# Operands fetched from DRAM by GpSimd's own transfers, and a work planner with durations read from a trace

## The chip, the cores and the metric

One core of one Trainium2 chip runs the whole program. The metric is the device time of one execution in microseconds (us); the time of a kernel is the median of its runs.

## The reference

Inputs are q, k, v of shape (4, 8, 576, 64) and six weights. All are float64 in DRAM; the kernel reads them as pairs of 32-bit words and makes float32 of them.

```python
scores = scale * q @ k.T + bias[h] * (-|i - j|), kept where 0 <= i - j < 128
attn   = softmax(scores);  x = (attn @ v), heads side by side: (4, 576, 512)
xn     = (x - mean(x)) / sqrt(var(x) + 1e-6) * g_ln
x      = x + relu(xn @ w_ch1) @ w_ch2            # 512 -> 2048 -> 512
h      = relu(x @ w_in)                          # 512 -> 1024
c      = conv over the sequence, 3 taps, one weight per channel, zero padded
out    = (h * sigmoid(c)) @ w_out                # 1024 -> 512
```

## The kernel before, in words

Attention runs first, in code written in its own order; neither it nor its order is touched. Everything behind it is put into a list of operations (`Plan.add`: engine, an assumed duration in ns, what is read and written). `Plan.issue` then simulates the list with those durations several times (`Plan.schedule`) and emits the best order it met. TensorE's operations stay in the order in which the program added them; the orders on VectorE (DVE), ScalarE (ACT), GpSimd (POOL) and the transfer queue of SyncE (SP) are the planner's. On the chip each engine goes through its own list strictly in order, so a waiting instruction holds up all behind it.

A float32 product is made of three fp32r products of a high and a low part (`PASSES`), so each operand exists as two parts: ACT writes the high part, DVE or POOL the rest. The tokens are in six groups of 384 columns. The stages after attention, by the time in the profile:

- **First layer, groups 0 and 1, about 148 to 289 us.** For each hidden block f of 128 (16 of them) TensorE makes 12 matmuls of the hidden layer (`plain_hidden`) and 12 of the projection of the block before (`project`). Meanwhile the last 20 of the 32 weight tiles are turned from float64 words into parts (`convert`, `convert_next`: one ACT and three DVE operations, ACT for the high and POOL for the low part) from a ring of three raw buffers. Between the blocks stand the statistics of later groups: `norm_turn` (four transposes of TensorE, two DVE operations) three times, then `norm_gather`: a small root on POOL (six instructions), a transpose of its result on TensorE, and a store to DRAM, from where `norm_spread` broadcasts it.
- **Groups 2 and 3 (s=1), then 4 and 5 (s=2).** Two groups and two hidden blocks make a superquad (`superquad`, eight for each s): a 2 by 2 product in seven products instead of eight ("P2" to "P7" in `QUAD`), each of six matmuls, with four places "F" at which waiting work (`fill`, mostly projections, six matmuls each) is put between them. The combined weights were stored in DRAM and stream back through nine slots of `r1` (`stream_record`). Behind each s, `second_half` makes the odd group's hidden blocks and projections. s=1 runs from about 289, s=2 from about 418 us.
- **Second layer, from about 513 us.** The same product in seven for w_in (`quad2`, 288 columns), gates on DVE and ACT, and the output products (`store_chunks`) as filling.

An operand comes back from DRAM by `fetch` (line 1251): SP transfers 256 KB into a staging buffer of `fa` (or of `h`), and ACT copies it to its place with type fp32r (line 1258). There are 96 fetches for the stream (`w1d`), 28 for w_in (`wind`) and 16 for w_out (`woutd`), 140 in all.

```python
plan.add("SP", 70, lambda: nc.sync.dma_start(stage(), src), [src], [key], nbytes=262144)
if eng == "S":
    plan.add("S", 590, lambda: S.activation(dst, stage(), AF.Copy), [key], [dst])
```

Lines named below: 989 a product of the plan, 952 and 959/967 a helper's ACT and DVE operations, 343/348/353 the three DVE steps of a conversion, 1031 and 1062 the transposes of `norm_turn` and `norm_gather`, 1052 to 1057 the root on POOL, 1157 the low part on POOL, 1258 the copy of `fetch`.

## Time and profile before

| | us |
|---|---|
| median of 3 runs | 745.91 (743.84 to 746.87) |
| the profiled execution | 745.31 |
| its span in the profile | 743.6 |
| TensorE (PE) busy in it | 716.6 |
| DVE / ACT / POOL busy | 536.8 / 476.1 / 145.8 |

Of the span and the execution's own time 1.7 us lie outside the span. PE's busy time is what its matmuls cover; the rest of the span is time in which PE waits. A view by engine says which instruction PE waited for; the time-ordered view of PE shows where.

### The profile page before, as it was taken

The page shows a single profiled execution, that of the slowest core. Times are in us where ns is not written, and L with a number is a line of the kernel's source. Part 1 is how long each engine was busy: PE and PEld are TensorE (multiplying, and loading weights), DVE is VectorE, ACT ScalarE, POOL GpSimd, SP SyncE. Part 2 cuts the span into 40 slices and gives each one's busy share as a digit, 9 for nine tenths or more (in the row PEclk, how much of TensorE's full clock was granted, in tenths as well). Part 3 has the DMA queues.
Part 4 walks back from the last instruction along what each step waited for, and adds up shares of the span by engine and source line. Part 5 has one row for each costly group of instructions (what it writes and reads, how often), then busy time and mean ns, then how long its engine had stood idle before and what let it go on. Part 6 is the DMA issues. An engine that isn't in the chain of part 4 may idle for free.

```text
span 743.6 us, 13429 instructions
## 1 busy us (share of the span) xinstructions
PE 716.6 (96%) x4704; PEld 667.4 (90%) x4704; DVE 536.8 (72%) x1073; ACT 476.1 (64%) x1190; POOL 145.8 (20%) x248
## 2 busy tenths in 40 slices
PE   8999998899899999999999999999999999999998
PEld 7777876799899999999999899999999898998887
DVE  5799999569999836555678665558468999687631
ACT  4888877545534435664556466677779977777742
POOL 1678789634631110000000000000000000000000
PEclk9999999999999999999999999999999999999999
DMA  6877765137759733877761388886704200000011
GB/s 152 183 169 172 198 157 150 42 91 220 235 186 319 226 119 100 284 263 257 227 222 40 117 275 292 290 258 206 227 15 143 86 15 29 30 29 15 29 43 57
DMA packets 122303, 114.63 MB, mean 154 GB/s; under 512 B 63552, under 2 KB 87292, under 8 KB 122236
## 3 DMA queue, kind: packets, MB, share of 16 engines
q1 hardware_dynamic: 121180, 113.52, 50.3%
q8 instruction: 37, 0.61, 0.3%
q10 hardware_dynamic: 1056, 0.26, 0.2%
q14 instruction: 30, 0.25, 0.1%
HBM read 80.70 MB, written 33.05 MB: 153 GB/s over the span
## 4 chain that ended last, share of the span: by engine, by line
PE 63%; DVE 3%; DMA 2%; ACT 2%; POOL 1%; issue 1%; SPq 0%; ACTq 0%; POOLq 0%; DVEq 0%
PE bank L989 63%; DVE fa L959 1%; DMA w1d<-r 1%; ACT fa L952 1%; DMA fa<-in_moe_w_out 1%; ACT r L1258 0%; PE bank L1031 0%; DMA h<-woutd 0%; DVE small L1039 0%; POOL small L1053 0%; DVE hhr L967 0%; DVE x L959 0%; DVE xn L967 0%; DVE xn L959 0%; DVE fa L353 0%
## 5 line engine op out<-in xcount | busy, mean ns | idle before, releaser
L989 PE MATMUL bank<-hhr,r 128*128 128x384 f32 x1152 | 214.5, 338 | 1.1 <-DVE fa L959 1.0
L989 PE MATMUL bank<-r,r 128*128 128x288 f32 (+1 forms) x1248 | 204.7, 315 | 5.2 <-ACT fa L952 4.3
L989 PEld LDWEIGHTS bank<-r,r 128*128 128x128 f32 x1248 | 193.8, 188 | 9.4 <-ACT fa L952 6.1
L989 PEld LDWEIGHTS bank<-hhr,r 128*128 128x128 f32 x1152 | 199.3, 188 | 2.3 <-DVE fa L959 1.7
L1258 ACT ACTIVATE r<-fa 128x512 fp32r<-128x512 f32 x115 | 70.6, 626 | 23.2 <-DMA fa<-w1d 9.7
L989 PE MATMUL bank<-r 128*128 128x512 f32 (+2 forms) x360 | 81.2, 370 | 0.3 <-ACT r L1258 0.3
L952 ACT ACTIVATE fa<-bank 128x288 f32<-128x288 f32 (+1 forms) x112 | 49.5, 442 | 38.1 <-PE bank L989 36.2
L989 PEld LDWEIGHTS bank<-r 128*128 128x128 f32 x360 | 64.0, 188 | 10.0 <-ACT r L1258 0.7
L989 PE MATMUL bank<-xn,r 128*128 128x384 f32 x360 | 68.5, 339 | 0.1
L989 PEld LDWEIGHTS bank<-xn,r 128*128 128x128 f32 x360 | 63.8, 191 | 0.4 <-POOL r L1157 0.4
L959 DVE TENSOR_TENSOR fa<-bank,fa 128x288 f32<-128x288 f32 (+1 forms) x88 | 43.6, 500 | 28.2 <-ACT fa L952 17.6
L732 ACT ACTIVATE pp<-ps,mn 128x128 f32<-128x128 f32 x144 | 51.2, 378 | 13.6 <-DVE mn L722 11.7
L952 ACT ACTIVATE hhr<-bank 128x384 fp32r<-128x384 f32 x46 | 22.5, 490 | 56.4 <-PE bank L989 56.0
L952 ACT ACTIVATE r<-fa 128x256 fp32r<-128x256 f32 (+2 forms) x94 | 47.6, 519 | 14.4 <-DVE fa L353 10.1
L967 DVE SCALAR_TENSOR_TENSOR fa<-fa,cw 128x576 f32<-128x576 f32 x64 | 51.1, 812 | 1.3 <-ACT fa L952 0.8
L1800 POOL MEMSET fa<- 128x1 f32 x12 | 0.8, 98 | 261.4 <-DVE fa L353 219.3
L744 POOL TENSOR_SCALAR pp<-pp,sm 128x128 f32<-128x128 f32 x72 | 42.8, 604 | 33.8 <-DVE sm L741 31.7
L766 POOL TENSOR_SCALAR_AFFINE_SELECT pt<-pc 128x512 f32<-128x512 f32 x72 | 46.9, 680 | 2.0 <-ACT pc L759 1.6
L707 PE MATMUL ps<-kt,qt 64*128 64x256 f32 x288 | 45.3, 410 | 2.0 <-ACT pp L732 1.7
L959 DVE TENSOR_TENSOR r<-fa,r 128x256 fp32r<-128x256 f32 (+1 forms) x74 | 37.7, 521 | 11.6 <-ACT r L952 9.0
L782 PE MATMUL po<-pt,rawv 128*64 128x128 f32 x544 | 37.9, 281 | 7.5 <-POOL pt L766 5.3
L989 PE MATMUL bank<-r,hhr 128*128 128x512 f32 (+1 forms) x192 | 44.5, 381 | 0.0
(135 smaller groups left out, 1086.6 us busy)
## 6 DMA issues: line engine op xcount, KB each, us to landing
fa<-w1d SPq DMA_DIRECT2D x96, 256.0 KB, 3.9
fa<-in_moe_w_ch SPq DMA_DIRECT2D x32, 512.0 KB, 4.7
w1d<-r SPq DMA_DIRECT2D x40, 256.0 KB, 3.1
wind<-r SPq DMA_DIRECT2D x28, 256.0 KB, 3.4
fa<-wind SPq DMA_DIRECT2D x19, 256.0 KB, 3.3
out<-h SPq DMA_DIRECT2D x17, 256.0 KB, 2.0
rawq<-in_q SPq DMA_DIRECT2D x32, 128.0 KB, 3.9
rawv<-in_v SPq DMA_DIRECT2D x32, 128.0 KB, 2.8
```

The source lines that it names most:

```text
L707: T.matmul(ps[:, h, u, :].rearrange("p (o j) -> p o j", o=2), lhs, rhs, start=i == 0, stop=i == 1,)
L732: S.activation(pp[:, u, h, :], sc[:, h, u], AF.Exp, bias=mn[:, h, u : u + 1], scale=-1.0, accum_out=sm[:, 0, i : i + 1],)
L744: (G if i % 2 else V).tensor_scalar(out=pp[:, i, :], in0=pp[:, i, :], scalar1=sm[:, 1, i : i + 1], scalar2=1.0, op0=ALU.mult, op1=ALU.mult,)
L766: G.affine_select(out=parts[:, i], in_=pc, compare_op=ALU.is_ge, fill=0.0, base=base, pattern=[[0, 4], [sign, P]], channel_multiplier=-sign,)
L782: T.matmul(po[h * D : (h + 1) * D, u, :], rvs[bl, pr][:, t - 1 + i, h, :], pt[:, i, 2 * u + h, :], start=i == i0, stop=i == 1,)
L952: "S", 160 + 0.84 * cols(out), lambda: S.activation(out, src, func, **kw),
L959: "V", 40 + 1.3 * cols(out), lambda: V.tensor_tensor(out=out, in0=a, in1=b, op=op),
L967: lambda: V.scalar_tensor_tensor(out=out, in0=a, scalar=sc, in1=b, op0=op0, op1=op1),
L989: T.matmul(out, lhs, rhs, start=start and n == 0, stop=stop and n == len(items) - 1, skip_group_check=True,)
L1258: plan.add("S", 590, lambda: S.activation(dst, stage(), AF.Copy), [key], [dst])
L1800: plan.add("G", 100, lambda hp=hp, c=c: G.memset(hp[:, c : c + 1], 0.0), [], [hp[:, c : c + 1]])
```

## The change

`fetch` becomes one transfer issued from GpSimd, straight from DRAM into the fp32r place. The planner gets other durations, more rounds, and due times that move an operation's needs earlier where the simulated PE stalled. The gathers stand one block later, and the turns of later groups further apart. The first eight converted tiles have a fourth raw buffer. The projection of the last blocks of group 1 and of group 3 becomes filling for the next superquad. The core of the diff:

```diff
-    def issue(self, rate=0.29, landing=1800, wait=200, rounds=6):
+    def issue(self, rate=0.29, landing=1800, wait=200, rounds=16):
...
-            at = {i: starts[i] for i in pe}
+            for i in pe:
+                push[i] *= 0.8
+            for a, b, i in stall:
+                push[i] += b - a
+            at = {i: starts[i] - push[i] for i in pe}
...
-            "V", 40 + 1.3 * cols(out), lambda: V.tensor_tensor(out=out, in0=a, in1=b, op=op),
+            "V", tt_ns(cols(out)), lambda: V.tensor_tensor(out=out, in0=a, in1=b, op=op),
...
-        plan.add("G", 1500, root, [keys], [keys])
+        plan.add("G", 2650, root, [keys], [keys])
...
-        raw = fav(n % 3 * 1024, 1024).bitcast(I32)
+        k = n % 4 if n < NRAW4 else n % 3
+        raw = fav(k * 1024 if k < 3 else 4608, 1024).bitcast(I32)
...
     def fetch(dst, src, key=None, stage=None, eng="S"):
...
-        plan.add("SP", 70, lambda: nc.sync.dma_start(stage(), src), [src], [key], nbytes=262144)
-        if eng == "S":
-            plan.add("S", 590, lambda: S.activation(dst, stage(), AF.Copy), [key], [dst])
...
+        plan.add("G", 1100, lambda: nc.gpsimd.dma_start(dst, src), [src], [dst], nbytes=262144)
...
-            for gg, f0 in ((1, 2), (2, 9)) if g == 0 else ((3, 0), (4, 5), (5, 10)):
-                if f0 <= f < f0 + GT:
-                    norm_turn(gg, f - f0, bank[7])
-                if f == f0 + GT:
+            for gg, at in ((1, (2, 3, 4, 6)), (2, (9, 11, 13, 15))) if g == 0 else (
+                (3, (0, 1, 2, 4)), (4, (5, 6, 7, 9)), (5, (10, 11, 12, 14))
+            ):
+                if f in at[:GT]:
+                    norm_turn(gg, at.index(f), bank[7])
+                if f == at[GT]:
                     norm_gather(gg, bank[7])
...
-            if last is not None:
+            if last is not None and (g, f) != (1, NF1 - 1):
...
-    for cs in ((0, 1), (2, 3)):
-        fill.append(lambda cs=cs: project(NF1 - 1, cs, False, True))
+    for f in (NF1 - 2, NF1 - 1):
+        for cs in ((0, 1), (2, 3)):
+            fill.append(lambda f=f, cs=cs: project(f, cs, False, f == NF1 - 1))
...
+            if p == 0:
+                fillers(len(fill) - 4)
...
-            for fn in second_half(3):
+            half = second_half(3)
+            for fn in half[:-4]:
                 fn()
+            fill += half[-4:]
```

**The gather of group 2 on PE.** bank_2367 to bank_2370 take the projection (hhr), bank_2371 and bank_2372 the hidden layer (xn), bank_2374 the transposes of the statistics (of x) and of the root's result (of small). Before, from the last turn on:

```order
L1031 MATMUL bank_2374<-ident,x 128x128 x4
L989 MATMUL bank_2367<-hhr,r_2363 128x384 x3
L989 MATMUL bank_2368<-hhr,r_2363 128x384 x3
L989 MATMUL bank_2369<-hhr,r_2363 128x384 x3
L989 MATMUL bank_2370<-hhr,r_2363 128x384 x3
L989 MATMUL bank_2371<-xn,r_2363 128x384 x12
L1062 MATMUL bank_2374<-ident,small 6x128
```

and now:

```order
L1055 MATMUL bank_2374<-ident,x 128x128 x4
L1008 MATMUL bank_2367<-hhr,r_2363 128x384 x3
L1008 MATMUL bank_2368<-hhr,r_2363 128x384 x3
L1008 MATMUL bank_2369<-hhr,r_2363 128x384 x3
L1008 MATMUL bank_2370<-hhr,r_2363 128x384 x3
L1008 MATMUL bank_2371<-xn,r_2363 128x384 x12
L1008 MATMUL bank_2367<-hhr,r_2363 128x384 x3
L1008 MATMUL bank_2368<-hhr,r_2363 128x384 x3
L1008 MATMUL bank_2369<-hhr,r_2363 128x384 x3
L1008 MATMUL bank_2370<-hhr,r_2363 128x384 x3
L1008 MATMUL bank_2372<-xn,r_2363 128x384 x12
L1086 MATMUL bank_2374<-ident,small 6x128
```

Between the last turn and the gather stood 24 matmuls; now 48 do. The other four gathers moved in the same way.

**The first superquad of s=2 on PE.** bank_2371, 2372 and 2373 take the seven products, the others projections. Before, the superquad had no filling:

```order
L989 MATMUL bank_2373<-r_62 128x384 x6
L989 MATMUL bank_2371<-r_2363,r_62 128x384 x12
L989 MATMUL bank_2372<-r_2363,r_62 128x384 x6
L989 MATMUL bank_2371<-r_2363,r_62 128x384 x12
L989 MATMUL bank_2372<-r_2363,r_62 128x384 x6
```

and now:

```order
L1008 MATMUL bank_2373<-r_62 128x384 x6
L1008 MATMUL bank_2371<-r_2363,r_62 128x384 x6
L1008 MATMUL bank_2367<-hhr,r_2363 128x384 x3
L1008 MATMUL bank_2368<-hhr,r_2363 128x384 x3
L1008 MATMUL bank_2369<-hhr,r_2363 128x384 x3
L1008 MATMUL bank_2370<-hhr,r_2363 128x384 x3
L1008 MATMUL bank_2371<-r_2363,r_62 128x384 x6
L1008 MATMUL bank_2372<-r_2363,r_62 128x384 x6
L1008 MATMUL bank_2371<-r_2363,r_62 128x384 x6
```

Four projections of group 3 that stood ahead of the superquad now stand in it, at its places F.

**POOL's queue at the head of the stream.** In before POOL has no transfers; small is the root of a gather, w1d a combined weight in DRAM, r_62 the tile of the slots. Now (the roots of groups 4 and 5 stand between fetches):

```order
L1279 DMA r_62<-w1d_5_2398 128x512
L1279 DMA r_62<-w1d_2_2395 128x512
L1076 TENSOR_SCALAR small<-small 128x3
L1077 TENSOR_TENSOR small<-small,mhalf 128x3
L1078 TENSOR_TENSOR small<-small 128x3
L1079 TENSOR_TENSOR small<-small 128x3
L1080 TENSOR_SCALAR small<-small 128x3
L1081 TENSOR_TENSOR small<-small 128x3
L1279 DMA r_62<-w1d_6_2399 128x512
L1279 DMA r_62<-w1d_1_2401 128x512
```

140 transfers moved from SP's queue to POOL's, and the 140 copies of line 1258 left ACT's.

## Rows read from the trace of the kernel before

**Rows 1.** The page: busy time, share of the span, instructions of each engine.

```profile
PE 716.6 (96%) x4704; PEld 667.4 (90%) x4704; DVE 536.8 (72%) x1073; ACT 476.1 (64%) x1190; POOL 145.8 (20%) x248
```

**Rows 2.** PE's waits, whole span: total us, times, longest us.

```profile
PE po L782 <- POOL pt L766: 5.3, 7, 1.3
PE bank L989 <- ACT fa L952: 4.3, 5, 1.3
PE bank L1062 <- POOL small L1057: 3.0, 3, 2.0
PE bank L989 <- DVE fa L959: 1.9, 3, 0.9
PE bank L989 <- ACT r L1258: 0.3, 1, 0.3
```

**Rows 3.** PE in order of time, first layer: start us, us, instructions [idle before].

```profile
167.35 0.27 PE L1062 MATMUL bank<-ident,small 128*6 128x128 f32 x1 [0.64 <-POOL small L1057]
...
196.12 2.24 PE L989 MATMUL bank<-xn,r 128*128 128x384 f32 x12
200.32 0.27 PE L1062 MATMUL bank<-ident,small 128*6 128x128 f32 x1 [1.96 <-POOL small L1057]
200.35 3.09 PE L989 MATMUL bank<-hhr,r 128*128 128x384 f32 x12
203.24 3.08 PE L989 MATMUL bank<-xn,r 128*128 128x384 f32 x12
206.16 2.25 PE L989 MATMUL bank<-hhr,r 128*128 128x384 f32 x12
...
255.98 0.27 PE L1062 MATMUL bank<-ident,small 128*6 128x128 f32 x1 [0.36 <-POOL small L1057]
...
297.05 2.35 PE L989 MATMUL bank<-r,r 128*128 128x384 f32 x12 [0.64 <-ACT fa L952]
```

**Rows 4.** Stretches: us, busy us of PE, PEld, DVE, ACT, POOL; granted clock, DMA share, GB/s.

```profile
180.00:200.00 20.00, 18.34 (x109) 17.66 (x107) 19.37 (x32) 10.18 (x19) 10.48 (x12) 1.00 0.73 217
...
200.00:205.00 5.00, 4.68 (x19) 4.68 (x20) 4.84 (x6) 2.53 (x5) 3.34 (x3) 0.66 0.79 245
...
460.00:480.00 20.00, 20.00 (x116) 20.00 (x116) 12.31 (x26) 14.11 (x30) 0.00 (x0) 1.00 0.88 288
...
560.00:580.00 20.00, 18.86 (x126) 18.18 (x125) 18.05 (x32) 18.44 (x38) 0.00 (x0) 1.00 0.48 141
```

**Rows 5.** DVE in order of time, start of the plan's work.

```profile
153.40 0.70 DVE L1039 BATCH_NORM_STATS2 small<-bank 128x6 f32<-128x512 f32 x1 [3.20 <-PE bank L1031]
```

**Rows 6.** PE and ACT in order of time, 420 to 588 us.

```profile
420.76 3.39 PE L989 MATMUL bank<-r,r 128*128 128x384 f32 x18 [0.58 <-ACT fa L952]
424.79 2.35 PE L989 MATMUL bank<-r,r 128*128 128x384 f32 x12 [0.64 <-ACT fa L952]
...
541.36 1.28 ACT L952 ACT_TABLE_LOAD   x1
...
543.68 1.05 PE L989 MATMUL bank<-r,r 128*128 128x288 f32 x6 [1.33 <-ACT fa L952]
...
575.25 3.49 PE L989 MATMUL bank<-r,r 128*128 128x288 f32 x24 [1.14 <-ACT fa L952]
...
583.15 1.86 PE L989 MATMUL bank<-r,r 128*128 128x288 f32 x12 [0.86 <-DVE fa L959]
...
587.64 0.98 PE L989 MATMUL bank<-r 128*128 128x512 f32 x3 [0.34 <-ACT r L1258]
```

**Rows 7.** Groups of instructions, DVE's of 300 to 600 us: busy us, mean ns, idle before.

```profile
L1258 ACT ACTIVATE r<-fa 128x512 fp32r<-128x512 f32 x115 | 70.6, 626 | 23.2 <-DMA fa<-w1d 9.7
...
L1157 POOL TENSOR_TENSOR r<-fa,r 128x512 fp32r<-128x512 f32 x20 | 27.7, 1388 | 41.8 <-ACT r L952 40.8 <-DMA fa<-in_moe_w_ch 0.9
...
L348 DVE SCALAR_TENSOR_TENSOR fa<-fa 128x512 int32<-128x512 int32 x15 | 10.3, 688 | 0.3
...
L343 DVE TENSOR_SCALAR fa<-fa 128x512 int32<-128x512 int32 x14 | 6.0, 425 | 5.0 <-ACT fa L333 5.0
```

**Rows 8.** SP's queue in order of time: one issue of a fetch (start us, us).

```profile
536.68 0.32 SPq L1256 DMA_DIRECT2D fa<-wind  x1
```

**Rows 9.** The page, DMA issues: count, KB each, median us to landing.

```profile
fa<-w1d SPq DMA_DIRECT2D x96, 256.0 KB, 3.9
```

More of the change, by code (lines that the diff above doesn't have):

```diff
@@ L77, in add, with schedule @@
         return i
-    def schedule(self, pe, at, succ, cost, rate, landing, wait):
+    def schedule(self, pe, goal, succ, cost, rate, landing, wait):
         ops = self.ops
         n = len(ops)
-        horizon = max(at.values()) + 1e5
+        horizon = max(goal.values()) + 1e5
         due = [0.0] * n
@@ L85, in schedule @@
             if ops[i]["eng"] == "T":
-                due[i] = at[i]
+                due[i] = goal[i]
             else:
@@ L118, in schedule @@
                 else:
-                    when = max(free.get(eng, 0.0), min(est[i] for i in items))
-                    soon = [i for i in items if est[i] <= when + wait]
+                    at = {i: max(est[i], dma - 3000) if ops[i]["nbytes"] else est[i] for i in items}
+                    when = max(free.get(eng, 0.0), min(at.values()))
+                    soon = [i for i in items if at[i] <= when + wait]
                     i = min(soon, key=lambda i: (due[i], i))
-                    if est[i] > when:
-                        now = [j for j in items if est[j] <= when]
+                    if at[i] > when:
+                        now = [j for j in items if at[j] <= when]
                         j = min(now, key=lambda j: (due[j], j))
-                        if when + ops[j]["ns"] <= est[i] + wait or due[i] > when + ops[j]["ns"] + 1500:
+                        if when + ops[j]["ns"] <= at[i] + wait or due[i] > when + ops[j]["ns"] + 1500:
                             i = j
-                    start = max(when, est[i])
+                    start = max(when, at[i])
                 if ops[i]["lock"]:
@@ L174, in issue @@
         best = None
+        push = {i: 0.0 for i in pe}
         for _ in range(rounds):
@@ L946, in two, with act_ns, tt_ns, stt_ns @@
         return sum(isinstance(a, list) or plan.known.get(a.tensor.name) == "sb" for a in aps) > 1
+    def act_ns(n: int, bank: bool = False):
+        return 182 + 0.79 * n if bank else 201 + 0.826 * n
+    def tt_ns(n: int):
+        return 150 + 1.045 * n
+    def stt_ns(n: int):
+        return 44 + 1.333 * n
     def act(out, src, func=AF.Copy, scale=None):
         kw = {} if scale is None else {"scale": scale}
+        ns = act_ns(cols(out), plan.known.get(src.tensor.name) == "bank")
         plan.add(
-            "S", 160 + 0.84 * cols(out), lambda: S.activation(out, src, func, **kw),
+            "S", ns + 90 * isinstance(scale, bass.AP), lambda: S.activation(out, src, func, **kw),
             [src] + ([scale] if isinstance(scale, bass.AP) else []), [out],
@@ L965, in stt @@
         plan.add(
-            "V", 40 + 1.38 * cols(out),
+            "V", stt_ns(cols(out)),
             lambda: V.scalar_tensor_tensor(out=out, in0=a, scalar=sc, in1=b, op0=op0, op1=op1),
@@ L1013, in convert @@
         m = cv if mid is None else mid
-        plan.add("S", 620, lambda: rescale(m, rp, S), [raw], [m])
-        plan.add("V", 580, lambda: to_f32(cv, rp, (0,), m), [m], [m])
-        plan.add("V", 690, lambda: to_f32(cv, rp, (1,), m), [raw, m], [m], lock=two(raw, m))
-        plan.add("V", 690, lambda: to_f32(cv, rp, (2,), m), [raw, m], [cv], lock=two(raw, m))
+        psum = mid is not None
+        plan.add("S", 650, lambda: rescale(m, rp, S), [raw], [m])
+        plan.add("V", 688 if psum else 490, lambda: to_f32(cv, rp, (0,), m), [m], [m])
+        for i, dst in ((1, m), (2, cv)):
+            plan.add(
+                "V", 684 if psum else 700, lambda i=i: to_f32(cv, rp, (i,), m), [raw, m], [dst],
+                lock=two(raw, m),
+            )
     smn = [0]
@@ L1142, in tile_kernel @@
     AHEAD = 6
+    NRAW4 = 8
     def convert_next():
@@ L1155, in convert_next @@
         plan.add(
-            "G", 1310,
+            "G", 1350,
             lambda: G.tensor_tensor(
@@ L1251, in fetch @@
     def fetch(dst, src, key=None, stage=None, eng="S"):
-        if key is None:
-            t = gen()
-            key, stage = t, lambda: t
-        plan.add("SP", 70, lambda: nc.sync.dma_start(stage(), src), [src], [key], nbytes=262144)
-        if eng == "S":
-            plan.add("S", 590, lambda: S.activation(dst, stage(), AF.Copy), [key], [dst])
-        else:
-            plan.add(
-                "G", 670,
-                lambda: G.tensor_scalar(
-                    out=dst, in0=stage(), scalar1=1.0, scalar2=1.0, op0=ALU.mult, op1=ALU.mult
-                ),
-                [key], [dst], lock=True,
-            )
+        plan.add("G", 1100, lambda: nc.gpsimd.dma_start(dst, src), [src], [dst], nbytes=262144)
     def w_sums(f0, f1, dst, keep, at=None):
```

14 lines of the change are left out of this document (7 added, 7 removed).

## The prediction

> **What bounds the kernel now.** I begin with the page: PE is busy 716.6 us of a span of 743.6 [rows 1], no other engine above 72%. At most 27 us can be won by waiting less, and nothing in the change makes a matmul shorter or drops one. So the next view is PE's list of waits [rows 2]. Its largest entry, 5.3 us on POOL's pt, belongs to attention, which the change does not touch. What it can reach are the 3.0 us at line 1062 (the transpose that waits for the root of a gather), the 4.3 us on ACT and 1.9 us on DVE at line 989, and the 0.3 us on the copy of a fetch. The third view, PE in order of time, tells where they are [rows 3, 6]; the fourth, busy time by stretch, which engine is full there [rows 4].
>
> In the first layer PE waits 0.64, 1.96 and 0.36 us for three gathers [rows 3]. The middle one costs more than its wait: the two groups of 12 matmuls behind it take 3.09 and 3.08 us where their neighbours take 2.24 and 2.25, and in the stretch 200 to 205 us the mean granted clock is 0.66 of full speed [rows 3, 4], which is a time at 1.2 GHz and a time at 2.4 GHz, after PE had idled 1.96 us. Later PE waits 0.64 us in the first superquad of s=1 [rows 3], 0.58 and 0.64 us in that of s=2, and 1.33, 1.14, 0.86 and 0.34 us between 543 and 588 us [rows 6], where ACT is busy 18.4 of 20 us and DVE 18.1 [rows 4].
>
> **The change part by part.** The sum is made against the profiled execution of 745.31 us; the median of the runs shown is 745.91, 0.6 above it, so I take the difference off the median.
>
> *Later gathers.* What can be won: the three waits, 2.96 us, and the slow clock behind the second, (3.09 - 2.24) + (3.08 - 2.24) = 1.69 us; together 4.65 us. The excerpt of PE's order shows 24 more matmuls between the last turn and the gather. PE makes 116 matmuls in 20 us in a stretch without a gap [rows 4], 172 ns each, so the root gets 4.1 us more, over twice the longest wait. What holds it back is DVE: 19.37 of 20 us busy in 180 to 200 us [rows 4]. A block costs PE 24 x 0.172 = 4.1 us; a block whose two tiles are still to be converted costs DVE twice a first step of 0.43 us and two two-input steps of 0.69 us [rows 7], 3.6 us, and the low part of the hidden block and the statistics on top. DVE paces this stage nearly as PE does, and if PE no longer waits for the gather it soon waits for a tile, unless DVE loses less time itself. It idled 3.20 us at the start [rows 5], and the fourth raw buffer gives it tiles to work on then; but the new order still has an early statistic that waits for PE. So not all of it: I take 3.5 us, between 0 (DVE takes all back) and 4.65.
>
> *Filling for the first superquads.* In s=2 the waits of 0.58 and 0.64 us are those of a superquad whose products follow each other with nothing between; the excerpt of the new order has projections there. The moved instructions are the same ones, and nothing before them waits for them. I take 1.1 of 1.22 us; in s=1, where filling was there already and one more block is added, 0.4 of 0.64. Bounds 0 and 1.86 for both.
>
> *The copies off ACT.* 140 copies of 626 ns [rows 7] are 88 us of ACT's work, but nearly all of it lay beside a busy PE: the list of waits puts only 0.3 us on a copy directly [rows 2]. The gain is where ACT is full, at 543 to 588 us. Of the waits there, 1.14 us (an evacuation of a bank queued behind other ACT work) and 0.34 us (a copy) go. The 1.33 us follow a table load of 1.28 us [rows 6], which stays; the 0.86 us are on DVE, which loses no work. I take 2.0 of 3.67 us; bounds 0 and 3.67. The issues leave SP's queue, 0.32 us each [rows 8]; PE never waits for SP by name, so I count nothing for that.
>
> *The transfers on POOL.* The trace has no transfer issued by POOL. The nearest rows for what one costs POOL are SP's issue of 0.32 us [rows 8] below and POOL's costliest 512-column instruction, 1.39 us [rows 7], above. As code running on POOL it is nearer the second, so I take 1.39: 140 times is 195 us on an engine that is idle from 300 us on but for a few small instructions. A superquad takes PE 66 matmuls, 11.4 us, and needs seven fetches, 9.7 us. For s=2, nine slots are filled ahead, and the other 47 have eight superquads, 91 us: POOL decides from 91 / 47 = 1.94 us a fetch on. Landing took 3.9 us from SP [rows 9]; a slot is reused nine products later, at least 8 x 6 x 0.172 = 8.3 us after it came free, so a landing of up to 6 us behind an issue stays hidden. Cost on the path: 0; it is a rival if the price is higher. A fetch now waits in POOL's queue for its slot and for the store of its data. Behind it stand the roots of groups 4 and 5, but the slots ahead of these are freed by blocks that PE does before the turns, so I count nothing.
>
> The Trainium skill has a rule against this change: SBUF — State Buffer, section SBUF: two separate sides, says that GpSimd cannot write the descriptors of its transfers while a VectorE instruction runs in a mode that takes both ports, and advises SP or ACT for such transfers. Here line 343 is such a candidate: 425 ns where the two-input steps of the same size take 688 [rows 7]. By that rule all 14 together hold POOL up by at most 6.0 us [rows 7], which its slack covers, and the sum would not change; no row shows a transfer being held.
>
> *What comes new.* All orders but PE's are made anew, over shorter distances, and a moved wait turns up elsewhere. I count two new waits of the mean size on ACT, 4.3 / 5 = 0.86 us [rows 2]: 1.7 us lost. Bounds 0 and the whole gain.
>
> Sum: 3.5 + 1.1 + 0.4 + 2.0 - 1.7 = 5.3 us; 745.31 becomes 740.0, and the median 745.9 becomes **740.6 us**.
>
> **The rivals.**
>
> (a) *All of it goes.* 4.65 + 1.86 + 3.67 = 10.2 us and nothing new: 735.7. For it: the new durations are near those of the rows (1.35 us for POOL's low part, 1.39 measured). Against: the table load and a DVE that is as full as before.
>
> (b) *DVE takes the place of the gather and of ACT.* It is at 19.37 and 18.05 of 20 us in the two stretches that matter [rows 4], and no DVE work is removed. Then only the filling stays, some 1.5 us: 744.4.
>
> (c) *POOL becomes the bound: slower.* Each issue would have to wait for a DVE instruction as well, one of 0.69 us on average: 1.39 + 0.69 = 2.08 us, above 1.94. In s=2 that is 47 x 2.08 - 91 = 6.8 us. For the 44 fetches of the second layer there are some 79 us, from the end of s=2 (about 509) to 588 us, where PE waits for such a fetch [rows 6]: 44 x 2.08 - 79 = 12.5 us. With the copies' gain gone and 5.0 us kept: 745.9 + 19.3 - 5.0 = 760. For it: DVE is 12 to 18 of 20 us busy then [rows 4], with two-input instructions mostly. Against: nothing measured says that an issue takes 1.39 us at all, or waits for DVE.
>
> (d) *The transfers themselves take twice as long,* because they now change the type on the way: slower. Seven of 256 KB in 11.4 us are 161 of 288 GB/s at a DMA share of 0.88 [rows 4]; doubled, the share would be 0.88 x 449 / 288 = 1.37, and eight superquads lengthen by 0.37 x 91 = 34 us: 775. No row bears on the type; that the same bytes move speaks against it.
>
> **How the numbers follow.** Half a per cent, 3.7 us, is about what a measurement of this kernel can tell from no change: 742.2 to 749.6. The forecast gets 0.52, its own range being 737 to 743 (half or all of the taken gains, with or without the new waits); 0.05 of that lies above 742.2. (a) gets 0.07, (b) 0.24, of which 0.03 is for losses beyond 749.6, (c) 0.12, (d) 0.05. Faster: 0.47 + 0.07 = 0.54; same: 0.05 + 0.21 = 0.26; slower: 0.03 + 0.12 + 0.05 = 0.20. The range of 735.5 to 750 takes in the forecast, (a) and (b), and leaves out (c) and (d), 0.17, and little else.
>
> **What would show it.** In the profile after: line 1062's wait (now another line) under 1 us in total and no dip of the granted clock near 200 us; no wait of PE on ACT in the first superquads; ACT near 476 - 88 = 388 us busy; POOL's transfers landing before PE asks. If DVE is the next bound, PE's waits in 160 to 220 us name DVE's conversions or POOL's low parts instead. The prediction is wrong if PE waits for transfers of POOL in s=1, s=2 or the second layer for more than 2 us in all, if those transfers land much later than 3.9 us after their issue, or if PE's busy time itself changes by more than 2 us.

## The result, and the profile after

Four runs each: the new kernel 739.66 us in the median (737.25 to 740.14), the kernel before 745.34 (743.84 to 746.87). The ratio is 0.9911 with a 95% interval of 0.9885 to 0.9937: faster, by 0.6 to 1.2 per cent. The profiled execution took 737.25 us at a span of 735.6. It is the fastest of the four, 2.4 us below the median, while that of the kernel before is at its median; so the 8.0 us between the two spans are more than the 5.7 us between the medians.

The page of the new kernel: busy time, share of the span and instructions of each engine (PEld is PE's loading of weights, which overlaps PE); the queues of SP's and of POOL's transfers (packets, MB, share of 16 engines); and one row of the DMA issues (count, KB each, median us to landing).

```profile
PE 711.3 (97%) x4704; PEld 664.1 (90%) x4704; DVE 534.2 (73%) x1073; ACT 404.4 (55%) x1050; POOL 223.3 (30%) x388
...
q1 hardware_dynamic: 101020, 76.81, 35.1%
q0 software_dynamic: 20160, 36.71, 18.5%
...
r<-w1d POOLq DMA_DIRECT2D x96, 256.0 KB, 4.8
```

The 36.71 MB on POOL's queue are the 140 fetches of 256 KB. Against [rows 1], ACT has 140 instructions and 72 us of busy time less, POOL 140 more and 78 us more, and a transfer lands 4.8 us after POOL's issue where SP's took 3.9 [rows 9]. DVE is as busy as before.

PE's list of waits (us in total, times, longest):

```profile
PE bank L1008 <- DVE fa L978: 1.7, 3, 0.9
...
PE bank L1008 <- DVE hhr L986: 1.0, 2, 0.8
PE bank L1008 <- POOL r L1183: 1.0, 1, 1.0
...
PE bank L1055 <- DVE small L1063: 0.8, 1, 0.8
```

No row names a fetch. Line 989 of the kernel before is line 1008 now, 1031 is 1055, 1062 is 1086, 1157 is 1183, 952 is 971, 959 is 978 and 967 is 986. The entry for the roots of the gathers, 3.0 us in [rows 2], is down to 0.4, and that for ACT at the products, 4.3 us, to 0.7. But DVE's statistics (line 1063), its low parts of the hidden block and POOL's low part stand in their place. PE in order of time tells where (start us, us, instructions, and the idle time before them with what ended it):

```profile
191.71 0.66 PE L1055 MATMUL bank<-ident,x 128*128 128x128 f32 x4 [0.82 <-DVE small L1063]
...
197.99 2.18 PE L1008 MATMUL bank<-hhr,r 128*128 128x384 f32 x11 [0.80 <-DVE hhr L986]
200.00 2.25 PE L1008 MATMUL bank<-xn,r 128*128 128x384 f32 x12
...
202.44 2.42 PE L1008 MATMUL bank<-hhr,r 128*128 128x384 f32 x12
...
211.55 0.27 PE L1086 MATMUL bank<-ident,small 128*6 128x128 f32 x1 [0.44 <-POOL small L1081]
...
213.13 2.00 PE L1008 MATMUL bank<-hhr,r 128*128 128x384 f32 x10 [0.96 <-POOL r L1183]
```

With one of 0.22 us behind the first row, the waits here come to 0.82 + 0.22 + 0.80 + 0.44 + 0.96 = 3.24 us. The three gathers cost 2.96 before [rows 3]. So PE waits no less in this stage; what is gone is the slow stretch: the stretch of 200 to 205 us (columns as in [rows 4]) is at full clock, 0.66 before, and PE is busy all of it; in no 5 us behind 125 us is the clock lower:

```profile
200.00:205.00 5.00, 5.00 (x31) 4.88 (x31) 4.40 (x9) 2.31 (x4) 2.86 (x2) 1.00 0.80 226
```

To set the stages of all runs side by side I take four marks from PE in order of time: the first product of the plan, the first with 288 columns, the first with 512 columns, and the end of the span. All products that the change moves stay within the second column. One profiled execution each; missing records can shift a mark by a few tenths of a us. "Limit" stands for a few lines of the planner that are part of the change and are told at e10; the excerpt of the change ahead of the prediction leaves them out.

| kernel | to the plan's start | to the first 288-column product | on to the first 512-column product | to the end | ratio to before, 95% |
|---|---|---|---|---|---|
| before | 148.5 | 378.6 | 51.5 | 165.0 | 1 |
| the change | 147.1 | 374.0 | 49.6 | 164.8 | 0.9911 (0.9885 to 0.9937) |
| the change again (e8) | 146.9 | 374.0 | 49.6 | 164.8 | 0.9917 (0.9885 to 0.9948) |
| e1, old fetch | 146.9 | 380.4 | 51.7 | 165.2 | 0.9976 (0.9957 to 0.9996) |
| e2, only the new fetch | 149.0 | 398.3 | 49.0 | 165.0 | 1.0189 (1.0162 to 1.0217) |
| e3, old gathers | 147.3 | 376.8 | 49.4 | 164.8 | 0.9929 (0.9903 to 0.9955) |
| e4, no filling | 146.6 | 378.9 | 49.6 | 164.8 | 0.9947 (0.9926 to 0.9968) |
| e5, planner only | 147.4 | 381.1 | 50.6 | 164.9 | 0.9990 (0.9968 to 1.0011) |
| e6, planner and fetch | 146.7 | 378.6 | 49.6 | 164.9 | 0.9963 (0.9941 to 0.9986) |
| e9, e2 with the root mostly on DVE | 146.9 | 394.4 | 49.5 | 163.4 | 1.0145 (1.0110 to 1.0179) |
| e10, before, new fetch, limit | 147.6 | 380.0 | 48.9 | 165.7 | 0.9958 (0.9934 to 0.9982) |
| e11, the change without limit | 148.4 | 386.6 | 49.4 | 164.9 | 1.0039 (1.0018 to 1.0059) |
| e12, three instructions before a fetch | 148.8 | 376.3 | 54.0 | 172.4 | 1.0082 (1.0050 to 1.0114) |
| e13, six of them | 148.2 | 431.8 | 74.2 | 192.9 | 1.1363 (1.1321 to 1.1404) |

Of the 8.0 us between the two spans, 4.6 lie in the second column and 1.9 in the third. The first column is attention, which no kernel here alters; it is 146.6 to 149.0 us in these executions, so its 1.35 us are taken as chance.

### The profile page after: what moved, and what is told of

Read it like the earlier page. It is cut to its first block, busy times and chain, and to the rows that moved or that the text cites. A ratio compares the mean times of both kernels' runs of the same rounds, so it can differ in the third digit from the quotient of the medians.

```text
span 735.6 us, 13436 instructions
## 1 busy us (share of the span) xinstructions
PE 711.3 (97%) x4704; PEld 664.1 (90%) x4704; DVE 534.2 (73%) x1073; ACT 404.4 (55%) x1050; POOL 223.3 (30%) x388
## 3 DMA queue, kind: packets, MB, share of 16 engines
q1 hardware_dynamic: 101020, 76.81, 35.1%
q0 software_dynamic: 20160, 36.71, 18.5%
## 4 chain that ended last, share of the span: by engine, by line
PE 67%; DVE 2%; DMA 1%; ACT 1%; POOL 1%; issue 0%; SPq 0%; ACTq 0%
PE bank L1008 66%; DMA fa<-in_moe_w_out 1%; DVE fa L978 1%; DMA fa<-in_moe_w_ch 1%; PE bank L1055 1%; DVE fa L986 0%; POOL r L1183 0%; ACT fa L971 0%; DVE fa L359 0%; DVE x L978 0%; ACT fa L339 0%; DVE h L1698 0%; DVE fa L354 0%; ACT L971 0%; POOL small L1077 0%
## 5 line engine op out<-in xcount | busy, mean ns | idle before, releaser
L1279 POOL DMA_DIRECT2D r<-w1d x96 | 51.4, 536 | 164.7 <-PE bank L1008 146.8
L788 PEld LDWEIGHTS po<-pt,rawv 128*64 128x64 f32 x544 | 29.5, 138 | 15.5 <-POOL pt L772 12.2
```

The lines of the kernel that those rows point to most:

```text
L788: T.matmul(po[h * D : (h + 1) * D, u, :], rvs[bl, pr][:, t - 1 + i, h, :], pt[:, i, 2 * u + h, :], start=i == i0, stop=i == 1,)
L1279: plan.add("G", 1100, lambda: nc.gpsimd.dma_start(dst, src), [src], [dst], nbytes=262144)
```

## The experiments

### One part undone: e1, e3, e4

**e1: the old fetch in the new kernel.**

```diff
-        plan.add("G", 1100, lambda: nc.gpsimd.dma_start(dst, src), [src], [dst], nbytes=262144)
...
+        plan.add("SP", 70, lambda: nc.sync.dma_start(stage(), src), [src], [key], nbytes=262144)
+        if eng == "S":
+            plan.add("S", act_ns(512), lambda: S.activation(dst, stage(), AF.Copy), [key], [dst])
...
```

> The new kernel (739.7 us), but operands are fetched as before: SP's transfer into a staging tile and a copy by ScalarE. Theory (each part brings its own few us: later gathers 2.3, copies off ScalarE about 2.7, filling about 1): ACT busy about 404 + 88 = 490 us, POOL about 140 x 0.54 = 75 us less, PE again waits for ACT after 540 us, and the time is 742 to 743 us, some 0.35% above the new kernel. Rival 1 (the new durations of the planner and the later gathers do it, the copies were hidden): within 0.7 us of the new kernel. Rival 2 (the copies carry the whole gain): 745 us, no better than the kernel before.

Measured: 0.9976, 0.6 per cent above the new kernel. ACT is busy 476.1 us. The third column of the table, where ACT is full, is 51.7 us against 49.6: 2.1 us more. The second column is 6.3 us longer, in two parts. Up to the first product of the first superquad it is 2.0 us, all of it before 220 us, where no fetch runs yet (the first copy is at 256.8 us): PE stands 4.05 us for DVE's low part, and the granted clock is 0.66 in 195 to 200 us.

```profile
196.43 1.97 PE L1008 MATMUL bank<-hhr,r 128*128 128x384 f32 x5 [4.05 <-DVE hhr L986]
```

The other 4.4 us lie in s=1 and s=2, where the copies run, with waits for DVE and ACT of up to 0.93 us. So both rivals fall: the copies were not hidden, and without the new fetch some gain is left (0.0004 to 0.0043 of the time). But taking the fetch back also makes every engine's order anew, and a part undone brings its own accidents; how much of the 4.4 us is the copies', this run does not tell.

**e3: the old places of turns and gathers.**

```diff
-            for gg, at in ((1, (2, 3, 4, 6)), (2, (9, 11, 13, 15))) if g == 0 else (
-                (3, (0, 1, 2, 4)), (4, (5, 6, 7, 9)), (5, (10, 11, 12, 14))
-            ):
+            for gg, f0 in ((1, 2), (2, 9)) if g == 0 else ((3, 0), (4, 5), (5, 10)):
...
```

> The new kernel with the statistics' turns and gathers where they were before. Theory: the wait for the second gather is back (about 2 us) and with it a granted clock below 0.8 in a stretch of some 5 us near 200 us: 742 us, 2.3 us above the new kernel. Rival (DVE sets the pace of the first layer and takes the place of the gather): the gather's wait is back, but waits for DVE's tiles go in exchange, and the time is within 0.7 us of the new kernel.

The diff shows that the gathers did not all move by one block: that of group 2 went from block 12 to block 15, since its turns stand further apart, the others by one.

Measured: 0.9929; its interval and that of the new kernel overlap for the larger part. From the plan's first product to the first of the first superquad it takes 136.7 us, the new kernel 136.9. The 2.7 us that the second column is longer all lie behind that, mostly in the superquads of s=2, with waits of 0.32 and 0.47 us that the new kernel has not; the gathers have no part in these, but the planner made their order anew too. Up to there PE waits 3.16 us in four places, 0.77 and 0.82 of them for the first two gathers, and the clock does not fall. The rival is right for the first layer: where the gather stands does not matter there, the waits are merely put down to someone else. Whether the gathers' places bring 1 us in the whole kernel, these runs cannot tell.

**e4: the moved filling undone.**

```diff
-            if last is not None and (g, f) != (1, NF1 - 1):
+            if last is not None:
...
-            half = second_half(3)
-            for fn in half[:-4]:
+            for fn in second_half(3):
...
```

> The new kernel without the moved filling: the last but one block's projections and the tail of the third second half stand where they stood before. Theory: the first superquads of s=1 and s=2 get back waits of some 0.6 us each, 1.0 to 1.8 us in all: 740.7 to 741.5 us. Rival (with the copies gone these superquads wait for nothing, filled or not): within 0.5 us of the new kernel, and no wait above 0.3 us in either superquad.

Measured: 0.9947, 0.3 per cent above the new kernel in 12 runs. PE in order of time has the three waits back, to the hundredth as in [rows 3] and [rows 6], now with ACT's line 971:

```profile
213.12 3.52 PE L1008 MATMUL bank<-hhr,r 128*128 128x384 f32 x10 [1.45 <-POOL r L1183]
...
295.47 1.83 PE L1008 MATMUL bank<-r,r 128*128 128x384 f32 x9 [0.64 <-ACT fa L971]
...
419.28 3.39 PE L1008 MATMUL bank<-r,r 128*128 128x384 f32 x18 [0.58 <-ACT fa L971]
423.31 2.00 PE L1008 MATMUL bank<-r,r 128*128 128x384 f32 x10 [0.64 <-ACT fa L971]
```

So the filling is worth the 1.86 us of these waits. The first row shows 2.0 us more that this execution lost: the wait for POOL's low part was 1.45 us instead of 0.96, and the ten products behind it took 3.52 us instead of 2.00, at a granted clock of 0.81 in 210 to 215 us. The second column is 4.8 us longer than the new kernel's; the last us of it is in no wait of the list.

### The planner and the fetch, each alone and together: e2, e5, e6

**e2: the kernel before with the new fetch, and nothing else.**

```diff
-        plan.add("SP", 70, lambda: nc.sync.dma_start(stage(), src), [src], [key], nbytes=262144)
...
+        plan.add("G", 1100, lambda: nc.gpsimd.dma_start(dst, src), [src], [dst], nbytes=262144)
...
```

> The kernel before (745.3 us) with one edit: fetches are POOL's own transfers, no copies on ScalarE; durations, rounds, gathers and filling as before. Theory: only the second layer gains, 2 to 3 us, the gather near 200 us keeps its wait of about 2 us and its slow clock: 742.5 to 743.5 us. Rival 1 (the copies were hidden): 745 us. Rival 2 (the copies carry the whole gain): 740 us. If POOL's transfers need the other parts of the change to be harmless (a transfer held up in POOL's queue behind a root), slower than 746 us with PE waiting for a fetch.

Measured: 1.0189, slower by 14 us, as the last of the expectations had it; but PE waits for a root, and no wait of it names a fetch. The third column has its gain, 49.0 for 51.5 us; the second loses 19.7 us. PE's list of waits and POOL in order of time (line 1062 and 1052 to 1057 are those of the kernel before, 1253 the fetch):

```profile
PE bank L1062 <- POOL small L1057: 15.1, 4, 11.9
```

```profile
227.94 0.79 POOL L1253 DMA_DIRECT2D r<-w1d  x1 [4.80 <-DVE fa L959]
235.49 3.01 POOL L1052 TENSOR_SCALAR small<-small 128x3 f32<-128x3 f32 x1 [6.75 <-DVE small L1040]
238.58 0.88 POOL L1053 TENSOR_TENSOR small<-small,mhalf 128x3 f32<-128x3 f32 x1
239.54 8.53 POOL L1054 TENSOR_TENSOR small<-small 128x3 f32<-128x3 f32 x1
248.15 0.19 POOL L1055 TENSOR_TENSOR small<-small 128x3 f32<-128x3 f32 x1
```

The root of the third gather starts on time and then takes 13.5 us where it takes 3 in the kernel before. One fetch stands ahead of it in the queue, but had been issued 7.5 us earlier: the queue did not hold it. Two explanations were left, and e9 below is for them. First the question which part of the change prevents this.

**e5: the planner's part alone** (durations, rounds, push, the limit; old fetch, gathers and filling, three raw buffers).

```diff
-    NRAW4 = 8
+    NRAW4 = 0
...
-        plan.add("G", 1100, lambda: nc.gpsimd.dma_start(dst, src), [src], [dst], nbytes=262144)
+        plan.add("SP", 70, lambda: nc.sync.dma_start(stage(), src), [src], [key], nbytes=262144)
...
```

> Only the planner's part of the change (measured durations, sixteen rounds, the push, the limit on early transfers): old fetches, old gathers, old filling, three raw buffers. Theory (run e3_old_gathers has the first layer as short with the old gathers as with the later ones, so its gain must come from the planner): the first layer shortens by 1.7 us, the second layer is as long as before, the first superquads keep their three waits of 0.6 us: about 1.7 us below the kernel before, ratio 0.998. Rival (the fourth raw buffer is what shortens the first layer): ratio 1.000, the gather's wait near 200 us of some 2 us with its slow clock is still there.

Measured: 0.9990, no difference that can be told. The second gather's wait is 0.56 us and the clock stays up, but PE waits 4.99 us in the first layer in six places. The theory fails: from the plan's first product to the first superquad it takes 141.0 us, 140.4 before. Only the third column is shorter, by 0.9 us, with the copies still on ACT.

**e6: the planner's part and the new fetch.**

```diff
-    NRAW4 = 8
+    NRAW4 = 0
...
-            if last is not None and (g, f) != (1, NF1 - 1):
+            if last is not None:
...
```

> The planner's part and POOL's transfers together; old gathers, old filling, three raw buffers. Theory (the new durations, of the root of a gather above all, 2650 for 1500 ns, are what makes POOL's transfers harmless): no wait above 2 us for a root, the second layer 2 us shorter than before: 1.7 + 2.0 = 3.7 us below the kernel before, ratio 0.995. Rival (the order of run e2_only_new_fetch went wrong by the transfers themselves, and the later gathers or the fourth buffer mend it): a root's wait of several us is back, ratio above 1.005.

Measured: 0.9963, 2.8 us below the kernel before. No root waits over 1.1 us; the second column is that of the kernel before, 378.6 us, the third has its 1.9 us. Against e5, which differs in the fetch alone, it is 2.5 us shorter in the second column and 0.9 in the third, and 2.0 us by the two ratios. So the fetch is harmless here and brings a gain of its own; gathers, filling and the fourth raw buffer together bring the 4.6 us of the second column. The fourth raw buffer was never undone alone.

**e8: the change again,** on the chip of e5, e6 and e9.

> The new kernel as it is, beside the others on this chip: ratio 0.991 of the kernel before; with the old gathers (run e3_old_gathers) it was 0.993, so if the later gathers bring 2 us or more this run must be below 0.991.

Measured: 0.9917, the same stages to a tenth of a us. It is not below 0.991, but the 2 us that it was to tell are 0.0027, and its interval (0.9885 to 0.9948) is wider: what the later gathers bring stays open.

### What makes the fetch harmless: e9, e10, e11

**e9: e2 with five of the root's six instructions on VectorE.**

```diff
...
-            G.tensor_tensor(out=a, in0=y0, in1=y0, op=ALU.mult)
-            G.tensor_tensor(out=a, in0=a, in1=ve, op=ALU.mult)
...
+            V.tensor_tensor(out=a, in0=y0, in1=y0, op=ALU.mult)
+            V.tensor_tensor(out=a, in0=a, in1=ve, op=ALU.mult)
...
```

> Run e2_only_new_fetch with five of the root's six small instructions on VectorE; the power alone stays on POOL. Theory (a stream of VectorE instructions with both operands in SBUF kept POOL's small instruction from its operands, 8.5 us for one that takes 0.2 us elsewhere): VectorE now has to stop for the power, so POOL gets in; the wait of 11.9 us falls below 2 us and the time to 744 to 747 us, ratio 0.997 to 1.001. Rival (POOL was busy with its own transfers, or the statistics came late): the wait stays above 8 us and the ratio near 1.019.

Measured: 1.0145. PE still waits 9.0 us at this place, and neither theory nor rival says why. POOL's power is done at 234.68; the rest of the root stands in DVE's queue behind some 9 us of sums.

```profile
233.72 0.96 POOL L1063 TENSOR_TENSOR small<-small,mhalf 128x3 f32<-128x3 f32 x1 [6.08 <-DVE small L1060]
...
243.91 0.17 DVE L1053 TENSOR_TENSOR small<-small 128x3 f32<-128x3 f32 x1
...
244.73 0.37 PE L1067 MATMUL bank<-ident,small 128*6 128x128 f32 x1 [9.01 <-DVE small L1056]
```

So the planner itself had put the sums first, as it does where it takes PE to stand still anyway. That leads to the code that chooses an engine's next instruction. In the kernel before it takes the instruction due first, and only then adds that a transfer cannot start before the transfers ahead of it are nearly done; with fetches on POOL, the whole queue stands still for that in the plan, and what follows on other engines is planned to suit. A few lines of the change, the limit, take that time into account in the choice. They hold for every transfer in the plan, the loads of tiles on SP's queue too. POOL in order of time shows what they do: in e2 the fetch of 227.94 us stands ahead of the third root, in e10, which is e2 with these lines, none:

```profile
229.73 0.20 POOL L1053 TENSOR_SCALAR small<-small 128x3 f32<-128x3 f32 x1 [10.40 <-DVE small L1041]
...
232.93 1.86 POOL L1254 DMA_DIRECT2D r<-w1d  x3
```

**e10: e2 with the limit.**

```diff
-                    when = max(free.get(eng, 0.0), min(est[i] for i in items))
-                    soon = [i for i in items if est[i] <= when + wait]
+                    at = {i: max(est[i], dma - 3000) if ops[i]["nbytes"] else est[i] for i in items}
+                    when = max(free.get(eng, 0.0), min(at.values()))
+                    soon = [i for i in items if at[i] <= when + wait]
...
```

> Run e2_only_new_fetch with one more piece of the change: the three lines of the planner that take into account, when it chooses the next instruction of an engine, that a transfer cannot start while earlier ones are still to be moved. Theory (without them the planner puts one fetch ahead of the third root in POOL's queue, believes PE will stand still there and fills VectorE with sums; with them the fetch stands behind the root): the wait of 11.9 us is below 2 us, the second layer is 2 us shorter than before, and the ratio is 0.996 to 0.999. Rival (the durations are what mends it, the root's price above all): the wait of several us stays, ratio above 1.01.

Measured: 0.9958, 17 us faster than e2 by these lines alone, without new durations. The third root takes 3 us again, and PE waits 0.26 us for it. That the planner's picture of a standing POOL is what misplaced the sums in e2 is read from its code and fits e9; no run shows it by itself.

**e11: the change without the limit** (the same lines taken back).

> The new kernel without those three lines. In POOL's queue one fetch then stands ahead of the third root again. Theory: PE waits 5 to 12 us for that root and the clock falls behind the wait: 746 to 756 us, ratio 1.00 to 1.015. Rival (with measured durations the planner needs no such care): within 0.7 us of the new kernel, ratio 0.991.

Measured: 1.0039, 9 us slower than the new kernel. The time is as expected, the place is not: the third root is in time, although a fetch stands ahead of it again (issued at 230.19 us), and the losses lie 20 to 40 us earlier, at the conversions of the first layer, before the first fetch. ACT waits for a tile's load and PE for ACT:

```profile
197.18 0.66 ACT L338 ACTIVATE fa<-fa 128x512 f32<-128x512 f32 x1 [2.11 <-DMA fa<-in_moe_w_ch]
...
198.41 0.62 PE L1007 MATMUL bank<-xn,r 128*128 128x384 f32 x2 [3.41 <-ACT r L970]
200.19 3.57 PE L1007 MATMUL bank<-xn,r 128*128 128x384 f32 x10 [1.17 <-POOL r L1182]
203.56 3.28 PE L1007 MATMUL bank<-hhr,r 128*128 128x384 f32 x12
```

Behind the 3.41 us the clock is 0.57 of full speed in 198 to 206 us. So both with the old durations and with the new, the limit is worth 9 to 17 us in a kernel whose POOL issues the fetches. Only in e2 does a root behind a fetch pay for its lack; in e11 it is the loads of tiles, and no run takes the limit away while SP issues the fetches, so that the 9 us come from POOL's fetches is not shown.

### The price of a fetch on POOL: e12, e13

The groups of POOL's instructions in the new kernel show what the trace of before did not:

```profile
L1279 POOL DMA_DIRECT2D r<-w1d x96 | 51.4, 536 | 164.7 <-PE bank L1008 146.8 <-DMA w1d<-r 6.6 <-DMA woutd<-r 5.7
```

A fetch keeps POOL 0.54 us, and 0.57 from issue to issue where nothing holds it (three take 1.72 us at 254.68). Small instructions ahead of each fetch raise that:

```diff
...
-        plan.add("G", 1100, lambda: nc.gpsimd.dma_start(dst, src), [src], [dst], nbytes=262144)
+        def slow():
+            for _ in range(3):
+                G.tensor_scalar(out=mhalf2, in0=mhalf2, scalar1=1.0, scalar2=1.0, op0=ALU.mult, op1=ALU.mult)
+            nc.gpsimd.dma_start(dst, src)
...
```

**e12: three of them.**

> The new kernel with three small POOL instructions (128x3, own tile) ahead of each of the 140 fetches; the planner does not know of them. A fetch then costs POOL about 0.54 + 3 x 0.28 = 1.38 us, the price that the prediction assumed. Theory (POOL decides from 1.94 us a fetch on): no change, within 1 us of the new kernel, ratio 0.991 to 0.993. Rival (every microsecond on POOL lies between a slot coming free and the product that needs it): 10 us or more slower.

Measured: 1.0082, 12 us slower than the new kernel: the theory's "no change" fails. The price is higher than meant, since each issue stands 0.36 us behind the instruction ahead of it; from 425.61 to 449.18 us fourteen issues are 23.57 / 13 = 1.81 us apart:

```profile
425.61 0.58 POOL L1284 DMA_DIRECT2D r<-w1d  x1
426.22 0.76 POOL L1283 TENSOR_SCALAR mhalf<-mhalf 128x3 f32<-128x3 f32 x3
427.34 0.59 POOL L1284 DMA_DIRECT2D r<-w1d  x1 [0.36 <-issue]
```

At this price no product of s=2 waits for a fetch, as 1.81 is below the 1.94 us of the prediction. The second layer loses, in three waits, and with its clock at 0.96 and 0.91 in 515 to 560 and 560 to 600 us:

```profile
543.32 1.78 PE L1010 MATMUL bank<-r,r 128*128 128x288 f32 x6 [3.00 <-DMA r<-wind]
...
589.42 0.94 PE L1010 MATMUL bank<-r 128*128 128x512 f32 x3 [2.46 <-DMA r<-woutd]
593.70 1.62 PE L1010 MATMUL bank<-r 128*128 128x512 f32 x3 [3.35 <-DMA r<-woutd]
```

POOL's first and last issue of the second layer, and then the first one of the new kernel:

```profile
501.41 0.58 POOL L1284 DMA_DIRECT2D r<-wind  x1
...
590.63 0.58 POOL L1284 DMA_DIRECT2D r<-woutd  x1 [0.36 <-issue]
```

```profile
489.85 0.53 POOL L1279 DMA_DIRECT2D r<-wind  x1 [2.61 <-PE bank L1008]
```

The 44 issues are 89.22 / 43 = 2.07 us apart, since the three small instructions take up to 1.37 us there instead of 0.76. That is above the limit of 79 / 44 = 1.80 us, which the prediction worked out for its rival only. And they begin 11.6 us later than in the new kernel: in s=2 POOL issued one fetch behind the other and handed its lag on. So this run tells of 1.8 to 2.1 us a fetch; the 1.38 us that it was to test stay untested.

**e13: six of them.**

> The same with six small instructions: about 0.54 + 6 x 0.28 = 2.22 us a fetch, above 1.94. Theory: POOL decides in s=2 and in the second layer, 47 x 2.22 - 91 = 13 us and 44 x 2.22 - 79 = 19 us, so about 772 us, and PE waits for fetches by name. Rival (the slots filled ahead take it up): below 750 us.

Measured: 1.1363, 848 us, 76 us above the expectation. The issues are 2.57 us apart where nothing else holds POOL, not 2.22. PE's list of waits:

```profile
PE bank L1010 <- DMA r<-w1d: 30.4, 18, 4.6
PE bank L1010 <- DMA r<-woutd: 21.4, 5, 6.7
PE bank L1010 <- DMA r<-wind: 19.1, 3, 12.8
```

The waits for fetches are 70.9 us; the expectation's formula gives (47 x 2.57 - 91) + (44 x 2.57 - 79) = 64. The other 39 us are PE's own busy time, 750.1 us for 711.3: the granted clock is 0.87 in 450 to 600 us and 0.82 in 600 to 720, where PE is busy 118.2 of 150 and 85.2 of 120 us. The formula for the waits holds within a tenth at the price measured; what a bound on POOL costs is half as much again.

No run here beats the new kernel; the nearest, e3, cannot be told from it.

## Why the prediction was right, step by step

The time of 739.66 us is 0.9 below the forecast of 740.6 and inside its range, and faster had the largest chance. The forecast took 5.3 us off; the medians differ by 5.7. That the sum came so near is in part luck: the terms were off in both directions, and the largest risk had no price in it.

*Later gathers, 3.5 us taken (0 to 4.65): mis-sized.* From the plan's first product to the first of the first superquad (148.49 to 288.92 us before, 147.14 to 284.05 now) the new kernel takes 140.4 - 136.9 = 3.5 us less, but 12 products, 12 x 0.172 = 2.1 us, have only been moved behind that mark; 1.4 us are left. They are about the slow clock behind the second gather. The three waits, 2.96 us, did not go: DVE and POOL's low part took them over, as rival (b) said. The prediction's price for DVE was too low: it took 0.43 and 0.69 us from 300 to 600 us [rows 7], where POOL is idle. In the kernel before, 160 to 225 us, with POOL's low parts beside it, DVE's steps in SBUF took:

```profile
L348 DVE SCALAR_TENSOR_TENSOR fa<-fa 128x512 int32<-128x512 int32 x9 | 10.2, 1138 | 0.2
L353 DVE SCALAR_TENSOR_TENSOR fa<-fa 128x512 int32<-128x512 int32 x9 | 8.8, 976 | 0.2
...
L343 DVE TENSOR_SCALAR fa<-fa 128x512 int32<-128x512 int32 x8 | 5.0, 625 | 0.5 <-ACT fa L333 0.5
```

The three steps of the other tile of each two, which goes through PSUM, took 0.68 to 0.69 us each. Together that is 4.8 us for a block's two tiles, not 3.6, where the block takes PE 4.1. And e3 has the same first layer with the old places, so it was not the gathers' places that kept the clock up, but an order whose waits there, 1.02 us at the longest, are shorter. Which part of the change makes that order no run here tells: e5 and e6, without filling and fourth buffer, have first layers of 141.0 and 139.9 us.

*Filling, 1.5 of 1.86 us: right, and all of it.* e4 has the three waits back in full. In the trace s=1 and s=2 gain more: from the first superquad to the first 288-column product it is 238.2 us before and 237.1 now with 2.1 us more work, 3.1 us; about 1 us of it is in no wait of the list.

*Copies off ACT, 2.0 us: right in the second layer, where it was counted.* The third column is 50.6 to 51.7 us in the three kernels with copies and 48.9 to 49.6 in those with the new fetch at its own price. But it came from other waits than the prediction took. The 1.14 us became 0.50 and the 0.34 us went; the 0.86 us of DVE are 0.88; and the 1.33 us behind the table load did not stay. The load takes 1.28 us as before, but now PE waits only 0.22 us:

```profile
533.78 1.28 ACT L971 ACT_TABLE_LOAD   x1
...
536.52 1.06 PE L1008 MATMUL bank<-r,r 128*128 128x288 f32 x6 [0.22 <-ACT fa L971]
```

In e5 and e1, with the copies on ACT, PE waits 0 and 0.52 us behind that load: ACT's order decides, not the copies alone. That the sum came out is luck. And the fetch is worth more than this term: taken back it costs 0.6 per cent, 4.9 us (e1), part of it in s=1 and s=2, where the prediction counted nothing. ACT's busy time fell by 72 us, not by 88: counted once where instructions overlap, a copy is 0.51 us of it.

*POOL's transfers, cost 0: right, with a price that was wrong.* I took 1.39 us as the nearer end of 0.32 to 1.39; it is 0.54. At 0.54 x 47 = 25 us of 91 there is room for three times as much, which is why rival (c) was out. At 1.8 to 2.1 us the kernel is 12 us slower, as e12 shows, so the conclusion hung on the size more than the text said. They land 0.9 us later than SP's did, and PE waits for none. Rival (d) fell as well: in 460 to 480 us the transfers move 289 GB/s, 288 before [rows 4], with the type changed on the way.

```profile
460.00:480.00 20.00, 20.00 (x117) 19.95 (x116) 10.41 (x23) 7.10 (x16) 6.34 (x12) 1.00 0.97 289
```

But the DMA share there is 0.97, 0.88 before. The page of the kernel before has one queue for all:

```profile
q1 hardware_dynamic: 121180, 113.52, 50.3%
```

The 36.71 MB that moved to POOL's queue now take 18.5% of 735.6 us, 136 us of all 16 engines. Before they took 50.3% of 743.6 us less the 35.1% of 735.6 us that the rest still takes, 116 us: now a sixth more. So the 16 engines are now nearly full in s=2. Whether the type or the queue does that, no run tells.

*New waits, 1.7 us lost: too small by itself.* Those of the first layer on DVE and on POOL's low part, not on ACT, come to 2.8 us. Taken together with the gathers' term, 3.5 - 1.7 = 1.8 us were forecast for it and 1.4 measured: two errors that nearly cancel.

*The roots behind the fetches, counted at nothing: right for the new kernel, for a reason that the prediction did not give.* It argued from the slots. e2 and e10 show that a few lines of the planner decide it, worth 17 us there; in the new kernel they are worth 9 (e11). The prediction passes them over as part of "all orders but PE's are made anew". This was its largest risk, and none of its rivals held it.

One of its own tests failed: PE's busy time changed by 5.3 us, not under 2. Of these, 1.6 us are in the first 20 us of the span, where the clock was 0.91 before and is 1.00 now (15.81 and 14.19 us busy) and which the change does not touch; the slow stretch near 200 us has another 1.7 us. Of the other 2 us about half lie in s=1 and s=2; what they are I cannot tell.

## What to carry to other kernels

When a planner or any list scheduler makes the orders, a moved transfer is priced by what the planner believes of it: look first at how its model treats an engine whose next instruction must wait, since the kernels with POOL's fetches and without that one rule were slower than the one before (e2, e11). A wait that is removed where another engine is nearly full turns up under that engine's name; count only what it leaves behind, such as a slow clock. Take an engine's prices from the stage that they are used for: DVE's steps were 1.4 to 1.7 times as long where POOL worked beside it. And before an engine is called idle enough, work out the largest price per instruction at each stage that it could bear, and take the smallest of these; and see whether a stage without rest hands its lag to the next.

## What the runs showed of the hardware

**POOL beside DVE.** In the new kernel, 160 to 225 us, the same two-input step takes 1.12 us in the mean with both operands in SBUF and 0.68 with one of them in PSUM:

```profile
L359 DVE SCALAR_TENSOR_TENSOR fa<-fa 128x512 int32<-128x512 int32 x9 | 10.1, 1123 | 0.2
...
L359 DVE SCALAR_TENSOR_TENSOR fa<-fa,bank 128x512 int32<-128x512 int32 x9 | 6.1, 683 | 0.4
```

Of the nine in the first row, the five that begin while a low part of POOL (two SBUF operands) is running take 1.19 to 1.68 us; the four that begin ahead of one or away from it take 0.68 to 0.69. The Trainium skill, SBUF — State Buffer, section SBUF: two separate sides, has the rule for it: a DVE instruction with two SBUF inputs and a POOL instruction that reads SBUF exclude each other, and the one that begins first keeps the ports to its end. The trace agrees.

In e2 something is seen that this rule does not tell. POOL's instruction of 128x3 (line 1054) that takes 0.19 to 0.53 us in the other gathers of that run took 8.53 us, while DVE ran some 20 instructions on operands in SBUF without a gap. It ended at 248.07 us, and DVE's first gap is there:

```profile
247.60 0.42 DVE L959 TENSOR_TENSOR xn<-fa,xn 128x256 fp32r<-128x256 f32 x1
248.21 0.43 DVE L959 TENSOR_TENSOR xn<-fa,xn 128x256 fp32r<-128x256 f32 x1 [0.19 <-ACT xn L952]
```

In the kernel before, POOL's root came through a like stream of DVE within 3 us, an instruction at a time. What makes the difference stays open; e9 was meant to settle it and met another wait (there POOL's power took 0.96 us beside such a stream). That DVE kept POOL out is a reading of these times, not shown by an experiment.

**The clock after a wait.** A wait alone does not tell whether the clock falls: after 1.96 us in the kernel before it fell to 0.66, after 4.05 us in e1 to 0.66, after 1.45 us in e4 to 0.81, after 3.41 us in e11 to 0.57; after 3.05 us in e10 and 1.40 us in e5 it stayed at 1.00. (These are means over stretches of 5 to 8 us, of time at 1.2 and at 2.4 GHz.)

**A fetch beside a busy DVE.** The prediction put the hold-up of descriptors by DVE, a rule of the same section of the Trainium skill, at 6.0 us in all. The issue takes 0.53 us in the median and 0.79 at the most of 140, so it hardly shows in POOL's time; whether it is in the longer landing, 4.8 for 3.9 us, no run here tells.
